# Sharing the last stage's weight loads and result stores between two DMA queues, with whole-row stores for 20 of 36 tiles

## The chip, the cores and the metric
The kernel runs on one core of one Trainium2 chip, in one launch. Its time is that of one execution on the device, in microseconds (us). Times are given as the median of several executions; the profile comes from one execution more, which has a time of its own.

## The reference
Three layers follow one another, all in float32:

```python
# attention with pooled keys and values: q, k, v [8 batches, 8 heads, 576, 64]
k_p = k.reshape(B, H, 72, 8, D).mean(axis=3)
v_p = v.reshape(B, H, 72, 8, D).mean(axis=3)
attn = softmax(q @ k_p^T / sqrt(D));  x = attn @ v_p        # -> x [4608, 512]
# dense layer with a rational activation: w_in [512, 2048], w_out [2048, 512]
h = x @ w_in
P = a[0] + a[1]*h + a[2]*h*h + a[3]*h*h*h
Q = 1 + |b[0]|*|h| + |b[1]|*h*h
x = (P / (Q + 1e-6)) @ w_out                                 # [4608, 512]
# soft mixture of 8 experts with 4 slots each: phi [512, 32], w1 [8, 512, 1024], w2 [8, 1024, 512]
logits = x @ phi
d = softmax(logits, axis=0);  slot_input = d.T @ x           # [8, 4, 512]
slot_out[e] = max(slot_input[e] @ w1[e], 0) @ w2[e]
out = softmax(logits, axis=1) @ slot_out                     # [4608, 512]
```

## The kernel before
The 4608 rows are 36 tiles of 128. A run is four tiles, so there are nine runs, and the dense layer goes through each run in eight pairs of 128-wide blocks of the hidden 2048. For each batch the keys and values are first pooled by matmuls (`pool_k` L471, `pool_v` L477, copies L484) from tiles of `kN` and `kH`, the first of them loaded for batch 0 into slots A and S (L462, L464); for later batches accumulating DMAs on GpSimd's queue pool them in DRAM (`summed`, L429). Scores (L518), the softmax and the second product (L581) follow, then the three-term products of the dense layer (L663 to L665) and the rational function, shared by VectorE, ScalarE and GpSimd (L677 to L701). L737 transposes the results, L754 copies them out of PSUM. Words of w_in and w_out are split into parts by `words` (L597 to L611).

The last stage has two functions. `experts()` (L833) makes the loads of the last stage: 16 of folded w_out blocks (`wod`, 256 KB each, L876), 10 half tiles of the expert weights (256 KB, L860) and 59 whole tiles (512 KB, L891), all on SyncE's queue (`nc.sync`). They need a free slot: the tags q, at, kp, vp, en, x, w, gt, A, S, kv and att name sets of buffers that the body also uses. `tail()` (L893) has the slots of the experts, the transposes of the w_out blocks (L881), the product with them (L959), the first expert layer (L1013), its transposes (L1027) and the second layer (L1045), which is made in two halves of 256 columns, `hf` 0 and 1. For each half the eight groups of matmuls of L1045 are followed by a scaling (`so`, L1089 or L1090), a sum over the groups (`pg`, L1091), a copy (`so4`, L1092), and then the combination: matmuls into `po` (L1106), a copy to an `o` buffer by ScalarE (L1113) or VectorE (L1114) and a store (L1117). A store takes 256 rows by 256 columns, so 256 KB in rows of 1 KB; 36 of them are issued, 18 for each half.

The order of all work is written out. `Plan.op` numbers each group of instructions as the kernel's functions call it (a task). `Plan.run` then emits the tasks one after another as the string `ORDER` (L67 on) names them: "2792,A:0" is task 2792, which takes slot 0 of tag A for its buffer; a letter a, b or c behind the number takes the first, second or third alternative engine of the task. Each engine and each DMA queue works through its own tasks in that order, and a task waits on its engine for all that it depends on, for the reader of the slot's last content too. Task numbers that the steps name: 41 to 44 load the four tiles of batch 0 (41 and 42 of keys, 43 and 44 of values), 45 the half tile; 46 to 48 are `pool_k`, 49 and 50 the copies of L484, 51 to 53 `pool_v`; 119, 126 and 133 load tiles of w_in; 2633 is a group of transposes (L737) of the last run, 2602 and 2632 are copies (L754) that free its bank; 2775 to 2830 are loads of the last stage; 2915 to 2918 are the four groups of the second layer for columns 0 to 255, 2919 to 2922 those for columns 256 to 511.

Of the kernel before, what the change touches and what calls it, by code (L numbers as in the profile page):

```python
# [8 lines left out]
F32 = mybir.dt.float32  # L9
# [3 lines left out]
AF = mybir.ActivationFunctionType  # L13
# [5 lines left out]
B, H, S, D = 8, 8, 576, 64  # L19
SP = 72  # L20
# [13 lines left out]
t_act = lambda n, ps=1, ap=0: (0.172 if ps else 0.205) + 0.085 * ap + 0.000833 * n  # L34
# [18 lines left out]
FILL, FILZ = 30, 0  # L53

# [13 lines left out]
0 1 38 41,A:0 36 2 42,A:2 3 140,kv:1 31 45,S:2 4 32 119,gt:4 5 43,A:1 6 7 8 9 10 11 46,h:0 47 44,A:0 141,gt:3 126,gt:7 55,U:1 142 71,q:1 143 144  # L68
120,t:1 48 145a,w:10 583,kv:1 121 133,kv:0 147,gt:6 584,gt:1 35 122 154,gt:0 51 87,U:2 49 587,gt:5 123 146a 127,gt:4 52 124b,w:9 125a 128a 50 129 53
130 56,h:1,st:1,at:0 54 586,gt:7 131,w:7 72,h:0,st:0,at:1 57 132 134,t:0 59 58 588,wk:0 135a 75 73 37 76 60 136 61 12 13 74 14 15 137 16 77 589 62  # L70
161,kv:0 138a,w:6 155,t:1 103,U:1 585,kv:1 63a 156a 168,gt:4 139 17 148,gt:3 613,q:2 78 18 64,wk:1,att:0 182,gt:2 19 149a 359 20 65a 590 597,q:1 33
79a 66,wk:1 157 591 88,h:0,st:0,at:0 592 150 67 82,wk:0,S:2 89 80,wk:1 83 158 68,r:0,x:1,x:0 81 91 159a,w:2 90 162,gt:0 104,h:1,st:3,at:1 92 69 151 93
160 593,wk:1 107 169,t:0 70 152,w:12 105 170a 108 153 84,r:0 106 163a 94 183,t:1 594 253,gt:3 109 171 95 175,gt:6 85 39 110 231,gt:1 184a 189,kv:1 595
247,gt:7 111a 905,q:0 21 185 596 96,wk:0,att:0 22 86 97 98,wk:1 23 164 99 24 114,wk:0,S:0 172 112,wk:1 115 100,r:0 165 113 186 237,kv:0
598,wk:1,wk:0,st:0,at:0 166b,w:4 101 173,w:13 102 25 176,gt:5 174 599 116,r:0 232,gt:2 601 600 177a 602 26 167 117 27 28 614,wk:0,wk:1,st:1,at:1
248,gt:4 118 233a 178 391,h:1 645,q:2 190,gt:0 179 249a 617 180,w:14 392 234 254,gt:6 181 615 238,t:0 618 393 616 603 250 239a 251 255a 394 240 619
263,gt:7 235 191a 415,h:0 256 395,S:0,A:2,U:0 196,gt:1 629,q:1 241 236 187,w:11 192 416 203,kv:0 396 188 367 620 375 242 417 40 397 398a 360 418 604
400a 399 605 243,wk:1,ks:0 420,A:0 401a 439,h:1 419,S:1,U:1 244a 193 421 245,wk:0 608,wk:1,att:0 422a 440 402 621a 246 403,r:0 441 194b,w:1 609 404
195 197,gt:2 405 29 424a 606,wk:1 442 257 198a 406 425 210,gt:3 607 423 407,r:0 630,wk:0,wk:1,st:1,at:0 444,A:1 408 463,h:0 853,q:1 633 443,S:2,U:2
252 199 409 426 464 446 631 634 445 632 610,wk:1,x:3,x:2 410 635 200 427,r:0 448 624,wk:0,att:0 447 611 217,gt:1 465 625 258 279,kv:1 201,w:0 428 449  # L80
269,gt:0 204,t:0 259,wk:0,ks:0 285,gt:5 636 205a 429 466 264,gt:4 430 265a 202 612 260 431,r:0 261,wk:0 266 30 468,A:3 622,wk:1 361 487,h:1 432 623
267 262 368 467,S:1,U:0 433 646,wk:0,wk:1,st:2,at:1 268 206 211,gt:2 488 470 647 212a 648 450 434 489 649 280,t:1 213 469 490 637 471 451,r:0 281a
626,wk:0 650 472 452 651 511,h:0 207 270,gt:7 473 286,gt:6 453 627 512 454 271a 628 455,r:0 272 638,wk:1,att:0 493,U:1 640,wk:0 362 513 456 641 273
639 34 474 457 642,wk:0 274 224,kv:0 458 208,w:15 275,wk:1,ks:0 214 643 209 475,r:0 644 514 218,gt:3 282 215,w:8 276 369 287a 411,wk:0,gt:0 476
517,U:2 283 413,wk:1,gt:4 216 412 652 414 288 492,A:2 277,wk:1 435,wk:0 311,gt:2 653 477 327,kv:1 225,t:0 284 278a 219 491,S:0 437,wk:1 363 478 436
220 479,r:0 459,wk:0,gt:7 438 221 226a 494a 461,wk:1,gt:1 222,w:3 460 227 496 462 654,wk:0,att:0 495 516,A:0 656,wk:1 228 535,h:1 657 223a 295,kv:0
655 289 515,S:2 658,wk:0 497a 290 229,w:5 301,gt:5 518 873,q:2 291,wk:1,ks:0 480 659 498 481 536 660 296,t:1 482 292 312,gt:6 230 519 293,wk:1 537
499,r:0 294 313a 500 520 483,wk:1 297a 501 302,t:0 485,wk:0 370 502 538 303a 298 484 304 486 299 540,A:3 854,wk:1,wk:0,st:1,at:0 521a 300 539,S:1,U:0
559,h:0 305 503,r:0 542 855 306 328,gt:3 560 504 317,gt:5 541 343,kv:0 857 856 383 561 329a 505 522 858 544 506 307,wk:0,ks:0 859 543 545 523,r:0 562
318,t:1 524 319a 525 677,h:1 308 314 546 320 678 315 564,A:1 321 316 563,S:0,U:1 333,gt:2 330 309,wk:1 323,wk:0,ks:0 322 331 310 566 526 507,wk:1,gt:5  # L90
349,kv:1 324 332 860 527,r:0 509,wk:0,gt:6 344,t:0 528 679 508 529 510 364 565 530 325,wk:0 680 371 326a 547,r:0 567 334,t:1 531,wk:0 568 682,A:2 548
# [1102 lines left out]
```

## Time and profile before

| | us |
|---|---|
| median of 3 runs | 778.95 |
| lowest and highest of them | 777.73 and 782.79 |
| the profiled execution | 774.41 |
| its span, first to last instruction | 772.6 |
| granted TensorE clock over the span | 0.991 |

The profile's first lines give busy time in the span: TensorE 732.3 us (95%), VectorE 657.0 (85%), ScalarE 597.1 (77%), GpSimd 472.2 (61%). PE is TensorE, PEld its weight loads, DVE VectorE, ACT ScalarE, POOL GpSimd; SPq is SyncE's queue. q1 is the DMA queue of SyncE's issues, q0 that of GpSimd's. A row gives, where it is a group of instructions, line, engine, operation, out<-in, shapes and count, then busy time and mean in ns, then the idle time ahead and what ended it. Where times are given, they count from the start of the span.

### The profile page before, as it was taken

Reading aid. Unit: us, or ns where it says so; the run is one execution under the profiler, and the core shown is the slowest. Engines: PE = TensorE matmul, PEld = TensorE weight load, DVE = VectorE, ACT = ScalarE, POOL = GpSimd, SP = SyncE. Lnnn points to the kernel's source line nnn. Section 1 sums busy time; section 2 is a strip of 40 time slices with the busy share of each in tenths; the row PEclk is TensorE's granted clock in tenths of the full one; section 3 lists DMA queues with packets and bytes.
Section 4 is the critical chain, followed back from the end, with each engine's and each line's share of the span. In section 5 each row is a group of like instructions: output and inputs, shape, how many; then the busy total and the mean of one; then the engine's idle time right before and its main releaser. Section 6 shows DMA issues by size and latency. Waiting matters only on the chain.

```text
span 772.6 us, 15833 instructions
## 1 busy us (share of the span) xinstructions
PE 732.3 (95%) x6297; PEld 545.6 (71%) x6297; DVE 657.0 (85%) x985; ACT 597.1 (77%) x998; POOL 472.2 (61%) x288
## 2 busy tenths in 40 slices
PE   8999989999999999999999999999999998899983
PEld 6787757768787876877687677768768766664442
DVE  4999999989999998999999899999999998862132
ACT  3689899968986987898798888878898977772122
POOL 1336756578885998677587868837775877520000
PEclk9999999999999999999999999999999999999997
DMA  9767667465545320101001010001000125999998
GB/s 353 275 216 240 163 194 235 86 108 102 116 65 108 83 54 2 42 1 44 2 8 42 2 63 28 1 16 36 14 2 1 42 97 181 353 334 387 399 354 298
DMA packets 40561, 99.41 MB, mean 129 GB/s; under 512 B 4152, under 2 KB 14392, under 8 KB 40424
## 3 DMA queue, kind: packets, MB, share of 16 engines
q1 hardware_dynamic: 37352, 86.02, 31.1%
q0 software_dynamic: 3136, 12.39, 9.4%
q8 instruction: 49, 0.80, 0.4%
q14 instruction: 24, 0.20, 0.1%
HBM read 84.76 MB, written 27.79 MB: 146 GB/s over the span
## 4 chain that ended last, share of the span: by engine, by line
PE 57%; DVE 19%; ACT 12%; DMA 4%; issue 3%; POOL 3%; SPq 0%; DVEq 0%; ACTq 0%; POOLq 0%
PE h L663 12%; PE h L665 11%; PE h L664 11%; DVE a L685 4%; PE sc L518 4%; PE pt L569 3%; PE av L581 3%; PE bank L711 3%; DVE r L699 2%; DVE a L701 2%; DVE u L697 2%; PE l L1013 2%; ACT r L696 2%; ACT s L677 2%; ACT a L679 2%
## 5 line engine op out<-in xcount | busy, mean ns | idle before, releaser
L663 PE MATMUL h<-xh,wh 128*128 128x512 f32 x576 | 241.7, 420 | 9.5 <-DVE a L685 3.9
L664 PE MATMUL h<-xl,wh 128*128 128x512 f32 x576 | 227.4, 395 | 0.1
L665 PE MATMUL h<-xh,wh 128*128 128x512 f32 x576 | 227.4, 395 | 0.0
L682 POOL TENSOR_TENSOR a<-a,s 128x1024 f32<-128x1024 f32 (+1 forms) x67 | 158.1, 2359 | 84.4 <-ACT s L677 57.6
L690 POOL TENSOR_TENSOR u<-u,s 128x1024 f32<-128x1024 f32 (+1 forms) x71 | 164.8, 2321 | 30.6 <-ACT s L687 25.5
L663 PEld LDWEIGHTS h<-xh,wh 128*128 128x128 f32 x576 | 108.3, 188 | 44.0 <-issue 7.8
L665 PEld LDWEIGHTS h<-xh,wh 128*128 128x128 f32 x576 | 108.3, 188 | 25.8
L664 PEld LDWEIGHTS h<-xl,wh 128*128 128x128 f32 x576 | 108.7, 189 | 19.4 <-DVE xl L586 0.5
L696 ACT ACTIVATE r<-s 128x512 f32<-128x512 f32 x144 | 87.1, 605 | 29.3 <-DVE a L701 28.6
L697 DVE SCALAR_TENSOR_TENSOR u<-u,r 128x512 f32<-128x512 f32 x144 | 96.9, 673 | 15.1 <-ACT r L696 14.2
L699 DVE SCALAR_TENSOR_TENSOR r<-a,cs,r 128x512 f32<-128x512 f32 x144 | 107.4, 746 | 0.0
L685 DVE SCALAR_TENSOR_TENSOR a<-h,cs,a 128x1024 f32<-128x1024 f32 (+1 forms) x75 | 92.7, 1236 | 10.3 <-ACT u L681 6.6
L701 DVE SCALAR_TENSOR_TENSOR a<-u,r 128x512 f32<-128x512 f32 x144 | 98.0, 682 | 3.2
L679 ACT ACTIVATE a<-h,cs 128x1024 f32<-128x1024 f32 (+1 forms) x73 | 85.8, 1176 | 9.7 <-PE h L665 9.5
L693 ACT ACTIVATE s<-u,cc 128x1024 f32<-128x1024 f32 (+1 forms) x75 | 84.1, 1121 | 7.7 <-POOL u L690 7.7
L688 POOL TENSOR_SCALAR s<-u,gb 128x1024 f32<-128x1024 f32 (+1 forms) x57 | 68.5, 1202 | 22.6 <-ACT u L681 12.4
L681 ACT ACTIVATE u<-h 128x1024 f32<-128x1024 f32 (+1 forms) x75 | 74.2, 990 | 8.0 <-PE h L665 3.4
L677 ACT ACTIVATE s<-h 128x1024 f32<-128x1024 f32 (+1 forms) x75 | 74.1, 989 | 5.6 <-PE h L665 5.1
L722 DVE STREAM_TRANSPOSE G<-a 128x1024 f32<-128x1024 f32 x56 | 69.3, 1238 | 0.1
L560 POOL TENSOR_TENSOR at<-at,st 128x576 f32<-128x576 f32 x31 | 36.9, 1192 | 22.5 <-DVE st L552 14.7
L537 ACT ACTIVATE at<-sc,st 128x72 f32<-128x72 f32 x192 | 45.4, 335 | 5.6 <-DVE st L531 5.2
L569 PE MATMUL pt<-ident,at 128*72 128x128 f32 x288 | 41.4, 273 | 3.6 <-DVE xl L586 1.5
(219 smaller groups left out, 1084.1 us busy)
## 6 DMA issues: line engine op xcount, KB each, us to landing
wx<-in_w SPq DMA_DIRECT2D x49, 512.0 KB, 5.9
qt<-in_qT SPq DMA_DIRECT2D x36, 256.0 KB, 2.9
out_dram<-o SPq DMA_DIRECT2D x22, 256.0 KB, 3.2
G<-in_w_in SPq DMA_DIRECT2D x10, 512.0 KB
G<-in_w_out SPq DMA_DIRECT2D x10, 512.0 KB, 5.6
G<-in_w SPq DMA_DIRECT2D x10, 512.0 KB, 8.1
wx<-wod SPq DMA_DIRECT2D x16, 256.0 KB, 4.0
ks<-in_kU POOLq DMA_DIRECT2D x7, 576.0 KB, 5.7
```

What stands on the lines that cost most here:

```text
L663: p_.matmul(o, w[:, 0, k], xh[r].t[:, k], start=(k == 0), stop=False)
L664: p_.matmul(o, w[:, 0, k], xl[r].t[:, k], start=False, stop=False)
L665: p_.matmul(o, w[:, 1, k], xh[r].t[:, k], start=False, stop=(k == 3))
L677: op("ACT", t_act(n), lambda fl=fl: a_.activation(out=fl(S_), in_=fl(h), func=AF.Square), [pt_(h)], [pt_(S_)], c, after=was("sq"), also=[A ...
L679: op("ACT", t_act(n, 1, 2), lambda fl=fl: a_.activation(out=fl(A), in_=fl(h), func=AF.Identity, scale=a3, bias=a2), [pt_(h), abt], [pt_(A) ...
L682: mul = lambda eng, fl=fl: eng.tensor_tensor(out=fl(A), in0=fl(A), in1=fl(S_), op=ALU.mult)
L685: op("DVE", t_dve(n, 1), lambda fl=fl: v_.scalar_tensor_tensor(out=fl(A), in0=fl(h), scalar=a1, in1=fl(A), op0=ALU.mult, op1=ALU.add), [pt ...
L690: mul = lambda eng, fl=fl: eng.tensor_tensor(out=fl(U), in0=fl(U), in1=fl(S_), op=ALU.mult)
L696: op("ACT", t_act(512, 0), lambda f=f, q=q: a_.activation(out=q.t, in_=S_.t[:, f], func=AF.Exp, scale=-1.0), [(S_, f)], [q], c + ky(r, "EX"))
L697: op("DVE", t_dve(512), lambda f=f, q=q: v_.scalar_tensor_tensor(out=U.t[:, f], in0=U.t[:, f], scalar=QC, in1=q.t, op0=ALU.add, op1=ALU.mult),
L699: op("DVE", t_dve(512, 1), lambda f=f, q=q: v_.scalar_tensor_tensor(out=q.t, in0=A.t[:, f], scalar=a0, in1=q.t, op0=ALU.add, op1=ALU.mult) ...
L701: op("DVE", t_dve(512), lambda f=f, q=q: v_.scalar_tensor_tensor(out=A.t[:, f], in0=U.t[:, f], scalar=-2.0, in1=q.t, op0=ALU.add, op1=ALU. ...
```

## The change
The change does four things. `wod` loads (L876), whole-tile loads (L891) and stores (L1117) get GpSimd's queue as an alternative to SyncE's. `FULL = 16`: for the row tiles from 16 on (20 of 36) the copies of both halves go into one `o` buffer [128, 2, 512] and the store is made once, in `hf` 1, as 512 KB in rows of 2 KB; the buffers live from the first half to the second. Their copies are split by 256 columns, so the 30 copies become 42, and the 36 stores become 26 (16 of 256 KB, 10 of 512 KB). L599 gets GpSimd as an alternative. And all of `ORDER` is replaced, by 3039 entries instead of 3037, of which the first difference is the third entry.

In the new order the alternatives are used as follows: 22 of the 59 whole-tile loads on GpSimd's queue and 37 on SyncE's, `wod` loads 0 of 16, L599 0 of 32, half-row stores 10 of 16, whole-row stores 6 of 10. The new numbers of the last tasks differ from the old ones, since there are more copies and fewer stores.

```diff
+FULL = 16
...
-0 1 38 41,A:0 36 2 42,A:2 3 140,kv:1 31 45,S:2 4 32 119,gt:4 5 43,A:1 6 7 8 9 10 11 46,h:0 47 44,A:0 141,gt:3 126,gt:7 55,U:1 142 71,q:1 143 144
...
-2689 2691,r:0 2633,wk:1 2855 2793,S:1 2692 2634 2856 2857 2776,w:5 2858 2693 2795,A:1 2663,wk:1,gt:6 2792,A:3 2690 2782,q:1 2694 2664 2665,wk:0,gt:5
...
+0 1 31 41,A:2 32 37 2 42,A:3 35 3 140,kv:1 45,S:0 4 38 43,A:0 5 36 6 7 8 9 10 11 12 13 46,h:1 141,gt:1 47 44,A:2 142 119,gt:3 126,gt:4 143 55,q:1 144
...
+2685 2633,wk:0 2661 2842 2792,A:0 2843 2687,wk:1 2662 2844 2735 2845 2846 2686 2744 2780a 2688 2847 2848 2776,w:5 2849 2691,r:0 2689 2795,A:1 2850
...
+2902 2906,U:0 2812a,gt:0 2907,wk:1 2815a,A:1 2915,r:0 2909,U:2 2910 2908 2821a,A:0 2894,m:1 2911,wk:1 2913,wk:0 2916 2912,U:2 2914 2917 2822a,gt:2
+2828,att:0 2918 2826a,gt:3 2919,wk:1 2945,t:0 2946,r:0 2825,kv:0 2920 2827,S:1 2947,t:1 2824,gt:5 2830,w:4 2984,wk:0,r:0 2829,A:0 2982,h:0 2986,w:14
...
-        op("ACT", 0.67, lambda: a_.activation(out=t.t, in_=raw.t[:, :, 1].bitcast(F32), func=AF.Abs, scale=2.0**-112), [raw], [t], key)
+        op("ACT", 0.67, lambda: a_.activation(out=t.t, in_=raw.t[:, :, 1].bitcast(F32), func=AF.Abs, scale=2.0**-112), [raw], [t], key,
+           alt=[("POOL", 1.25, lambda: g_.tensor_scalar_mul(t.t, raw.t[:, :, 1].bitcast(F32), 2.0**-112), False)])
...
-                    op("SP", SPI, lambda o=o, f=f: nc.sync.dma_start(out=o(), in_=wod[f].t), [wod[f]], [(b, part)], key, nbytes=128 * 2048)
+                    put = lambda eng, o=o, f=f: eng.dma_start(out=o(), in_=wod[f].t)
+                    op("SP", SPI, lambda put=put: put(nc.sync), [wod[f]], [(b, part)], key, nbytes=128 * 2048, alt=[("POOL", 1.0, lambda put=put: put(nc.gpsimd), False)])
...
-                op("SP", SPI, lambda o=o, src=src: nc.sync.dma_start(out=o(), in_=src), [], [(b, part)], key, nbytes=128 * 4096)
+                put = lambda eng, o=o, src=src: eng.dma_start(out=o(), in_=src)
+                op("SP", SPI, lambda put=put: put(nc.sync), [], [(b, part)], key, nbytes=128 * 4096, alt=[("POOL", 1.0, lambda put=put: put(nc.gpsimd), False)])
...
+        whole = {}
...
-                    o = buf(["w", "gt"], [128, 2, n, 256], "o", np_=2)
+                    full = g >= FULL
+                    if full and hf == 0:
+                        whole[g, jj] = buf(["w", "gt"], [128, 2, 512], "o", np_=4) if n == 1 else [buf(["w", "gt"], [128, 2, 512], "o", np_=4) for _ in range(2)]
+                    o = whole[g, jj] if full else buf(["w", "gt"], [128, 2, n, 256], "o", np_=2)
...
+                        if full:
+                            for m in range(n):
+                                oo = lambda i=i, m=m, os=os, po=po, cols=cols: os[m].t[:, :, cols] if len(po) == 1 else os[m].t[:, i, cols]
...
+                                op("ACT", t_act(w // n), lambda oo=oo, pm_=pm_: a_.activation(out=oo(), in_=pm_(), func=AF.Copy), [po[i]], [prt], kk,
+                                   alt=[("DVE", t_dve(w // n), lambda oo=oo, pm_=pm_: v_.tensor_copy(oo(), pm_()), False)])
+                            continue
...
+                        if full:
+                            if hf == 1:
+                                put = lambda eng, o=os[m], r0=r0: eng.dma_start(out=out[r0 : r0 + 256, :].rearrange("(j p) d -> p j d", p=128), in_=o.t)
+                                op("SP", SPI, lambda put=put: put(nc.sync), [os[m]], [], kk, nbytes=128 * 4096, alt=[("POOL", 1.0, lambda put=put: put(nc.gpsimd), False)])
+                            continue
+                        put = lambda eng, o=o, m=m, r0=r0, cols=cols: eng.dma_start(out=out[r0 : r0 + 256, cols].rearrange("(j p) d -> p j d", p=128), in_=o.t[:, :, m])
+                        op("SP", SPI, lambda put=put: put(nc.sync), [o], [], kk, nbytes=128 * 2048, alt=[("POOL", 1.0, lambda put=put: put(nc.gpsimd), False)])
```

## Rows read from the trace of the kernel before

**Rows 1.** The page's 40 equal slices: DMA busy tenths, and GB/s.

```profile
DMA  9767667465545320101001010001000125999998
GB/s 353 275 216 240 163 194 235 86 108 102 116 65 108 83 54 2 42 1 44 2 8 42 2 63 28 1 16 36 14 2 1 42 97 181 353 334 387 399 354 298
```

**Rows 2.** Busy time by stretches; PE, PEld, DVE, ACT, POOL, clock, DMA share, GB/s.

```profile
28.00:140.00 112.00, 105.94 (x798) 80.00 (x796) 107.69 (x169) 102.25 (x165) 61.77 (x43) 1.00 0.68 208
140.00:580.00 440.00, 433.25 (x3800) 332.77 (x3800) 411.95 (x606) 374.09 (x639) 334.01 (x188) 1.00 0.20 44
660.00:680.00 20.00, 16.99 (x140) 13.40 (x139) 16.37 (x26) 15.85 (x29) 12.03 (x10) 1.00 0.86 315
678.00:678.60 0.60, 0.60 (x19) 0.41 (x17) 0.46 (x1) 0.60 (x2) 0.41 (x1) 1.00 0.00 0
680.00:700.00 20.00, 19.27 (x186) 13.82 (x188) 13.32 (x30) 12.29 (x29) 1.43 (x3) 1.00 1.00 383
700.00:740.00 40.00, 36.48 (x377) 16.99 (x369) 6.35 (x13) 8.27 (x17) 0.00 (x0) 1.00 1.02 391
766.00:772.60 6.60, 0.00 (x0) 0.00 (x0) 0.00 (x0) 0.00 (x0) 0.00 (x0) 0.50 0.69 231
```

**Rows 3.** The chain that ended last, from 740 us: start, us, what.

```profile
735.99 8.60 DMA wx<-in_w
744.64 3.64 PE lo L1045 x58
...
749.34 1.86 PE lo L1045 x32
```

**Rows 4.** Timeline of SyncE's queue: start, us, line, operation, count.

```profile
671.87 1.28 SPq L891 DMA_DIRECT2D wx<-in_w  x3
...
678.13 0.80 SPq L891 DMA_DIRECT2D wx<-in_w  x2
```

**Rows 5.** The chain that ended last, from 0 to 60 us.

```profile
10.16 2.81 PE pk L477 x4
13.06 0.41 ACT kp L484
13.51 2.43 PE pk L477 x4
...
17.50 1.19 PE sc L518 x8
...
32.32 1.73 PE pv L477 x4
```

**Rows 6.** Timeline of ScalarE, TensorE and GpSimd near 680 us.

```profile
678.73 0.59 ACT L754 ACTIVATE G<-gp 128x512 f32<-128x512 f32 x1
...
681.74 0.66 PE L737 MATMUL gp<-ident,a 128*128 128x128 f32 x4 [0.37 <-ACT G L754]
...
678.91 1.27 POOL L690 TENSOR_TENSOR u<-u,s 128x512 f32<-128x512 f32 x1 [0.51 <-ACT s L687]
```

**Rows 7.** Timeline of GpSimd: the issue of one DMA.

```profile
143.83 1.06 POOL L429 DMA_DIRECT2D vs<-in_vS  x1
```

**Rows 8.** DMA queue by window 724:737, 764:770, 151.2:152.4: packets, MB, share.

```profile
q1 hardware_dynamic: 1444, 5.26, 101.6%
...
q1 hardware_dynamic: 2133, 2.05, 102.6%
...
q1 hardware_dynamic: 129, 0.23, 51.4%
```

**Rows 9.** VectorE's timeline at 754 us, and copies of 735:773 by line and shape.

```profile
754.24 1.29 DVE L1114 COPY o<-po 128x512 f32<-128x512 f32 x2 [0.55 <-PE po L1106]
...
L1114 DVE COPY o<-po 128x1024 f32<-128x1024 f32 x2 | 2.5, 1225 | 1.7 <-DMA wx<-in_w 1.7
L1114 DVE COPY o<-po 128x256 f32<-128x256 f32 x2 | 0.8, 416 | 0.0
L1113 ACT ACTIVATE o<-po 128x256 f32<-128x256 f32 x2 | 0.8, 380 | 1.1 <-PE po L1106 1.1
```

**Rows 10.** Page, DMA queues over the span: packets, MB, share of 16 engines.

```profile
q1 hardware_dynamic: 37352, 86.02, 31.1%
q0 software_dynamic: 3136, 12.39, 9.4%
```

More of the change, by code (lines that the diff above doesn't have):

```diff
@@ L72 @@
[L72 to L79, printed above, removed]
@@ new lines @@
+71,U:0 587,gt:2 145a,w:10 583,kv:1 133,kv:0 48 584,gt:5 146 51 120,gt:0 121 122 14 127,t:0 52 123 49 50 128 147,gt:3 124b,w:6 129 53 125a
+56,h:0,st:0,at:1 54 130 154,gt:0 87,U:1 72,h:1,st:1,at:0 131a,w:13 57 58 588,wk:1 59 134,gt:6 132 75 73 135a 76 74 60 589 77 161,kv:1 136 61 137 62
+138a,w:8 585,kv:0 103,q:1 155,gt:7 168,gt:4 63a 15 148,t:1 182,gt:1 139 16 78 17 149a 18 156 64,wk:0,S:1 79a 590 65a 19 591 20 150 66,wk:0 592 157
+88,h:1,st:2,at:1 67 158 82,wk:0,S:0 91 80,wk:1 159a,w:15 586,gt:0 83 89 68,r:0,x:2,x:3 359 92 169,t:0 39 90 81 160 151 104,h:0,st:3,at:0 93 69
@@ new lines @@
+593,wk:0 597,q:1 162,gt:5 231,gt:7 105 152,w:7 70 163a 107 153 84,r:0 106 170a 108 94 109 594 33 85 110 95 183,t:1 86 595 184a 175,gt:0 164 237,kv:0
+21 613,q:0 111a 596 96,wk:1,att:0 22 97 185 98,wk:0 23 171 99 114,wk:1,S:1 115 112,wk:0 172 100,r:0 113 165 247,gt:4 186 189,kv:1
+598,wk:0,wk:1,st:2,at:0 101 166b,w:9 253,gt:1 176,gt:3 167 102 24 173,w:12 25 601 116,r:0 232,gt:2 599 602 174 177a 600 26 117 27
+614,wk:1,wk:0,st:1,at:1 248,gt:5 118 233a 28 178 391,h:1 249a 179 238,t:0 234 190,gt:6 392 615 180,w:1 617 254,gt:0 616 181 393 618 239a 250 191a
@@ new lines @@
+218,gt:4 369 411,wk:0,gt:1 476 225,t:0 283 276 517,U:0 216 413,wk:1,gt:6 652 295,kv:0 412 311,gt:5 288 414 284 653 492,A:0 477 277,wk:1 435,wk:0 278a
+219 491,S:1 437,wk:1 363 478 436 220 479,r:0 459,wk:0,gt:3 438 221 226a 494a 222,w:4 461,wk:1,gt:2 460 495 496 654,wk:0,att:0 462 516,A:2 227 656,wk:1
+535,h:1 228 655 289 327,kv:1 657 497a 229,w:5 658,wk:0 515,S:2 223a 291,wk:1,ks:0 498 480 518 301,gt:4 290 481 536 659 375 312,gt:7 482 292 660
+296,t:1 293,wk:1 537 230 499,r:0 519 294 297a 483,wk:0 500 370 302,t:0 317,gt:0 313a 501 485,wk:1 520 303a 538 502 484 298 486 304 540,A:3
@@ new lines @@
+670 715,r:0 747,S:0,A:3,U:0 716 671 717 748 672 718 374 732 697 673 750 719 674 733,r:0 749 675 765,h:1 734 676 766 752 735 698,gt:0
+874,wk:1,wk:0,st:1,at:0 753 736 767 877 875 664 876 768 377 878 751 879 890,wk:0,wk:1,st:3,at:1 771,U:1 872 880 787,h:0 769,S:2,A:0 891 881 893
+737,r:0 892 788 894 770 738 720,gt:1 895 882,wk:1,att:0 772 884,wk:0 883 789 739 885 754 740 906,wk:1,wk:0,st:2,at:0 896 755,r:0 790 1149,q:2 774a 897
+909 1133 910 1115,q:0 907 1130,ks:0 886,wk:0 773 775 792,A:2 741 908 791,S:1,U:2 756 898,wk:1,att:0 911 757 809,h:1 794 899 758 887 912 900,wk:1 810
@@ new lines @@
+1126a 962 1124 824 946 786,gt:4 825,r:0 1127,wk:0,x:1,x:0 945 826 963 1128 827 842 380 1129 964 828 948 947 843,r:0 1150,wk:0,wk:1,st:2,at:1
+965,S:0,A:0,U:0 949 844 983,h:1 966 1140 1151 984 845 1152 1141 1153 846 985 1154 808,gt:5 968 847,r:0 986 967 848 849 950 1144,wk:0,att:0 807 850 970
+1145 969 829 987,S:2,A:2,U:1 971 851 852,gt:7 951,r:0 1142,wk:0 921 1005,h:0 924a,L:0 1143a 988 952 1146,wk:0 922,m:0 972 953 990 954 1006 830,gt:6
+955,r:0 1147 1007 381 956 923 1148 989 387 991 927,wk:1 928,wk:0 1008 930 992 929,en:0 957 958 931,h:1,wk:1,wk:0 1010,kv:0 993 1155 932 973,r:0
@@ new lines @@
+1528 1475 1451 1493,r:0 1442 1452 2925 1510 1454 1543,h:1 1453 1527 1494 1681,wk:1,wk:0,st:3,at:0 2926 1530 1544 1904,q:1 1495 1664 1935 1682 1531
+1545 1684 1683 1496 1529 1511,r:0 1546 1685 1512 1675,wk:1,att:0 1686 1549,U:1 1673,wk:0 1565,h:0 1513 1676 1687 1532 1674a 1566 1514 1547,S:2,A:1
+1498,gt:1 1677,wk:1 1515,r:0 1548 1516 1567 2927 1937 1678 1550 348 1517 1476,gt:0 1568 1518 1497 1679 1552 1533,r:0 1519 1551 1571,U:2
+1890,wk:1,wk:0,st:2,at:1 1553 1570,A:3 1534 1587,h:1 1535 1569,S:1 1893 1536 1588 1894 1572 1891 1520,gt:2 1537,r:0 1589 1892 1538 1554 1574 1539
@@ new lines @@
+1690,wk:0,att:0 1688,wk:1 1691 1540 1590 1689 1575 1573 1555,r:0 1692,wk:1 1592,A:0 1556 1542,gt:3 1609,h:0 1591,S:0,U:0 1895 1936a 1594 1610 1693
+2192,ks:0 1593 1557 1919,q:2 1694 1611 1558 1896 1595 1559,r:0 1612 1596a 1560 1576 1905,wk:1,wk:0,st:0,at:0 1561 1597 1562 1713,h:1 1614,A:2
+1564,gt:4 1577,r:0 1714 1613,S:2,U:1 1578 1908 1615 1616 1906 1715 1579 1909 1580 1541 1598 1563 1617 1618 1581,r:0 1897,wk:0,att:0 1716 1898 1582
+1619 1907 1583 1899,wk:0 1584 1735,h:0 1900 1910 1599,r:0 1718,kv:0 1901,wk:1,x:2,x:3 1600 1911 1601 1717,S:1,U:2 1736 1602 1902 1720 1586,gt:5
@@ L203 @@
+2990,h:1 3010a 3031a 3009a 2991a,gt:6 3012a 3020,h:0 3011 2994,r:0,wk:0 3022,w:13 3021,gt:4 2996a,w:4 2974,h:0 2995a 3032,h:1 2997 3035,r:0,wk:1 3033a
+2998 3037 2975a 2976a 3023a 3036a 3024 3003,wk:0,r:0 3002 3034a 3004,w:2 3005a 3038a 3006 2993 3007a 2992a
 """
```

233 lines of the change are left out of this document (105 added, 128 removed).

## The prediction

> **What bounds the kernel now.** I read the page's 40 slices first, for the one engine that is not busy throughout: the DMA engines work hard in the first third, are nearly idle through the middle, and run at nine tenths or more over the last eight slices, some 150 us [rows 1]. Then busy time by stage: up to 680 us TensorE leaves 6.06 us of 112 and 6.75 us of 440 free, so the body is bound by compute, with the DMA engines at a fifth. From 680 us on it turns over: DMA share 1.00 and more, 383 and 391 GB/s, while the other engines run out of work [rows 2]. The chain that ended last says the same: it waits 8.60 us for a weight tile that lands at 744.6, does the last matmuls of the second expert layer, and everything behind is copies and stores [rows 3]. In SyncE's queue I then look for the place where the loads stop being issued: three 512 KB loads go out by 671.87 + 1.28 = 673.15, the next two at 678.13 [rows 4]. At 678.0 to 678.6 nothing was moved at all, 0 GB/s [rows 2]. So three things set the time: the compute up to 680, the moment at which the bulk of the weights can start, and the bytes from there to the last store.
>
> **Head.** The new order issues the load of the first value tile of batch 0 (task 43) fifth and no longer sixth, and moves the first 512 KB tile of w_in (119) behind it. TensorE began on that tile at 10.16 us, and the three groups of `pool_v` then set the chain to the scores at 17.50 [rows 5]. 512 KB fewer in front at the 353 GB/s of the first slice [rows 1] are 524,288 B / 353 GB/s = 1.49 us: −1.5. At best the first two groups also shrink to the 1.73 us that four such matmuls take at 32.32: 2.81 + 2.43 − 2 × 1.73 = 1.8 more, −3.3, rounded to −3.5. At worst the gain is eaten because the ACT copies of L484 now stand behind one group more, two of 0.41 us [rows 5]: +0.8, rounded to +1. I take −1.5, since what follows is chained to the scores.
>
> **Body, 28 to 660 us.** The whole order of 3037 entries is replaced, yet the same instructions stay on nearly the same engines: the new POOL alternative of L599 is used 0 times in 32, L688 goes from 57 to 60 on POOL, L601 from 3 to 5 on DVE, and so on by twos and threes. TensorE's idle time is all there is to win here, 6.06 + 6.75 us [rows 2], and a fresh order can lose as much as it wins. I take 0, with half of the first figure, ±3, as bounds.
>
> **Where the loads start again.** Before, the loads issued up to 673.15 came to 13.0 MiB; the queue went on at 678.13 [rows 4]; that sum is counted along the order. In the new order SyncE issues 12.75 MiB up to a like point and then stands at task 2792, whose slot A:0 is freed by task 2633, a group of transposes (L737) that ended at 681.74 + 0.66 = 682.4 before [rows 6]. There it had waited for an L754 copy; its bank in the new order is free after the L754 copy that ended at 678.73 + 0.59 = 679.3, so it can end near 680. What SyncE carries behind 2792 waits with it. GpSimd's queue doesn't help earlier: its first load of this part (2780) stands behind its last compute, which ended at 678.91 + 1.27 = 680.2 [rows 6]. So the restart is some 680 against 678.13, and the bytes left are 23.25 MiB against 23.0 (0.26 MB at 375 GB/s = 0.7 us). Were the engines dry in between, this costs 1.9 + 0.7 = 2.6; loads still in flight cover a part, as they did before until shortly ahead of 678.0. I take +2.0; below, 0, if the loads issued later than I think cover it; above, +5.0, with A:0 as late as before (4.3 + 0.7).
>
> **The bulk of the weights.** Before, 23.0 MiB = 24.1 MB landed between 679 and 744.6, 368 GB/s over all, in stretches of 383 and 391 [rows 2]; 375 between them is my rate for both kernels, 65 us. Twenty-two of the 59 loads of 512 KB move to GpSimd's queue. Its compute is over by then, so nothing waits there but stores. The issue itself costs 1.06 us on GpSimd [rows 7] against about 0.4 on SyncE (0.80 for two, [rows 4]); 22 × 1.06 = 23 us lies inside 65 and beside SyncE's. Stores of the first half of the columns, seven of eight, also go through GpSimd, and the last loads (2822, 2826) stand behind matmuls in the same queue: +0.5, between 0 and three issues of 1.06 us, +3. Before, one queue already filled the engines (101.6% share at its best, 406 GB/s over 13 us, [rows 8]), so a second queue adds no bandwidth that the rows show.
> The Trainium skill ("DMA: Bandwidth & Descriptors" in its section "Issuing engines are not separate DMA queues") says that transfers issued by several engines run on the same 16 DMA engines, and that issuing from several saves only sequencer time. That speaks against any gain from the sharing; by that rule the sharing is worth 0 here, against the −4.9 us of the first rival below, and the trace's full share with one queue agrees.
>
> **After the last weight.** Before, from the last landing (744.64) to the end of the span (772.6) it was 28.0 us; the first copy for the second half of the columns ran from 754.24 on DVE, its store could go out at 755.0 [rows 9]. Stores of the first half covered the gap. Now only 16 of 36 tiles store half rows in the first half (8 × 256 KB = 2.1 MB); the other 20 keep both halves in ten buffers and go out once as ten stores of 512 KB. Behind the last landing I count: last group of the second layer, 32 matmuls, 1.86 us; 751.2 to 755.0 for the scaling, the group sum and the first combination, 3.8 [rows 3, 9]; about 0.9 from issue to bytes (after the issue of 678.13 nothing had moved by 678.6 [rows 2, 4], so over 0.5); together 6.6, in which 2.1 MB of first-half stores take 2.1 / 342 GB/s = 6.1 [rows 8] and just fit. Then 8 × 256 KB at 342 = 6.1 and 5.24 MB in 2 KB rows. Their price: at 342 GB/s as 1 KB rows 15.3 us, at 406 as the 4 KB weight rows [rows 8] 12.9; I take 376 between, 13.9. Then 2.1 us from the last bytes to the end, as before: the share of 0.69 of the last 6.60 us [rows 2] is 4.5 us of transfers, to 770.5. 6.6 + 6.1 + 13.9 + 2.1 = 28.7 against 28.0: +0.7. The whole rows save about 1.4 us of transfer, and moving 2.6 MB of stores from the covered gap behind it takes more than that back. Twelve more copies (416 and 380 ns for 256 columns, 1225 ns for 1024 at once, [rows 9]) amount to a few us on two engines and lie beside 20 us of stores. Should they come first, each costs 0.4 us.
>
> **Sum.** −1.5 + 0 + 2.0 + 0.5 + 0.7 = +1.7. The profiled execution took 774.41 (span 772.6 and 1.8 around it), which makes 776.1; the median of the three runs lies 4.5 above the profiled one, and I give the time beside that: 778.95 + 1.7 = 780.6.
>
> **The rivals.**
> Two queues move more than one. For: in two windows one queue made 383 and 406 GB/s [rows 2, 8], so the mean is not the ceiling. Against: the share is at 1.00 in both. 24.4 MB at 406 instead of 375 take 60.1 instead of 65.0 us, −4.9: 775.7. With no lag at the restart either it would be 773.7.
> The other side, slower: GpSimd's queue moves a byte slower than SyncE's. The only rows for it are the accumulating loads of the pooling, 12.39 MB for 9.4% of 772.6 us = 72.6 us of all engines, 171 GB/s [rows 10] (q1: 86.02 MB for 31.1%, 358 GB/s). 17.3 MB move over (22 loads, 16 stores). At 171 they take 101.2 us instead of 46.1 at 375: +55, 836 us. They add to what lies in DRAM, which plain loads don't, and that speaks against taking the figure over; half way, 273 GB/s, is +17, 798 us. It decides from about 331 GB/s down (+6.1, over 1%).
> A:0 comes as late as in the trace of before, 682.4: +3.0 on the forecast, 783.6.
> The new order of the body wins or loses the half of TensorE's idle time, 6 us: 774.6 or 786.6.
> The change doesn't do what it says: 2 KB rows cost per byte what 1 KB rows cost, the 1.4 us go: 782.0. The one stretch with such rows, 0.23 MB at a share of 51.4%, is too short to exclude it [rows 8].
>
> **How the numbers follow.** Forecast 0.46; two queues faster 0.16; GpSimd's queue slower 0.12; late slot 0.10; body 0.10 (either side half); dear 2 KB rows 0.06. One per cent is 7.8 us, about what a measurement of this kernel can tell from no change. Under 771.2 come 0.05 of the forecast (head and start at their good ends), 0.07 of the two queues and 0.05 of the body: 0.17. Over 786.7 come 0.09 of the slow queue, 0.03 of the body, 0.04 of late slot and forecast: 0.16. The rest, 0.67, is within 1%. The range: the terms' good ends (−3.5, −3, 0) with part of the faster queues reach to 769; their bad ends (+1, +3, +5, +3, not all at once) to 789. Outside lie the slow queue below some 320 GB/s and a combination of all good ends, about 0.2.
>
> **What would show it.** TensorE's scores first at about 16 and no longer 17.50. SyncE's queue with a pause from 672 to between 679.5 and 682, and a DMA share of 660 to 680 of some 0.73 instead of 0.86. q0 (GpSimd's) at 29.7 MB and its share: near 17.3 MB / 375 added, 46 us or 6%, on the 9.4%; clearly more would be the slow queue. Last weight at 746 to 747; first whole-row store some 10 us after it; span about 774.3. The forecast is wrong if the DMA rate from 680 on leaves 360 to 390 GB/s, if PE idle from 28 to 660 changes by over 3 us, or if the tail behind the last weight is not 27 to 31 us.

## The result and the profile after

| | before | changed |
|---|---|---|
| median of 5 runs, us | 778.95 (777.0 to 782.79) | 782.74 (779.24 to 783.91) |
| ratio to the kernel before, 95% interval | | 1.0053 (1.003 to 1.0076) |
| measured again later, 6 runs of the changed kernel | 777.98 | 784.15; 1.0073 (1.0051 to 1.0094) |
| profiled execution; span, us | 774.41; 772.6 | 782.74; 780.8 |
| granted TensorE clock | 0.991 | 0.976 |

The changed kernel is slower by 0.5 to 0.7%, some 4 to 6 us, which is within 1%. One execution in all the experiments, of the old head with the changed rest, took 1437.62 us and is left out of its ratio. The two profiled executions stand 8.2 us apart, more than the medians: the one of before lies 4.5 us under its median. So the split by stages below is of 8.2 us, and how much of each part is the kernel and how much the luck of one execution is what the experiments are to tell.

Page of the changed kernel, 40 slices and the DMA queues, against [rows 1, 10]:

```profile
DMA  8657587564536230101011010000200024989989
GB/s 321 237 199 238 128 240 246 122 112 87 114 67 125 55 82 2 28 1 36 23 43 41 2 49 1 1 29 15 71 2 14 15 83 135 376 325 399 403 301 326
...
q1 hardware_dynamic: 27112, 68.71, 25.3%
q0 software_dynamic: 7968, 29.69, 15.3%
```

The first slices move less than before (321 and 237 GB/s, before 353 and 275), and the last slice but one has a dip to 301 where [rows 1] has 354. q0 carries 17.3 MB more, as counted, and its share of the engines' time grows from 72.6 us (9.4% of 772.6) to 119.5 (15.3% of 780.8): 46.9 us, 369 GB/s, near the 375 that I took for SyncE's queue. So the rival with the slow queue is out at once.

Busy time by stretches of the changed kernel (columns as in [rows 2]):

```profile
28.00:140.00 112.00, 106.30 (x777) 80.96 (x778) 103.55 (x167) 96.64 (x157) 59.98 (x43) 0.96 0.70 216
140.00:580.00 440.00, 433.77 (x3755) 334.35 (x3762) 412.51 (x606) 374.22 (x641) 336.11 (x191) 1.00 0.22 47
...
684.00:688.00 4.00, 4.00 (x38) 4.00 (x38) 3.56 (x6) 3.94 (x8) 3.10 (x3) 1.00 0.28 77
...
700.00:740.00 40.00, 39.26 (x416) 19.43 (x418) 8.92 (x24) 10.28 (x22) 9.62 (x19) 1.00 1.02 402
...
752.00:756.00 4.00, 3.48 (x40) 1.96 (x32) 1.39 (x3) 2.00 (x6) 2.05 (x3) 1.00 0.56 196
756.00:760.00 4.00, 3.58 (x34) 2.68 (x34) 2.95 (x7) 1.70 (x5) 1.52 (x3) 1.00 0.72 255
```

TensorE is as busy in the body as before (433.77 of 440 against 433.25), but its clock from 28 to 140 is 0.96 instead of 1.00. The gap in the loads near 678 is now near 686 (share 0.28). And from 752 to 760, where the stores should run, the engines lie idle for 0.44 × 4 + 0.28 × 4 = 2.9 us; before, the shares there were 0.96 and 1.03:

```profile
752.00:756.00 4.00, 3.09 (x36) 2.12 (x36) 2.05 (x4) 2.43 (x4) 0.00 (x0) 1.00 0.96 319
756.00:760.00 4.00, 3.10 (x41) 2.26 (x36) 1.38 (x2) 3.40 (x6) 0.00 (x0) 1.00 1.03 343
```

The chain that ended last, first in the head (against [rows 5]), then at the end (against [rows 3]):

```profile
1.36 5.29 PE bank L390 x26
6.65 5.96 PE pk L472 x40
12.62 3.61 PE pk L478 x4
...
16.45 1.73 PE pk L478 x4
...
20.21 1.19 PE sc L519 x8
...
735.26 7.04 DMA G<-in_w
...
742.35 1.91 PE lo L1049 x26
744.26 4.25 PE po L1114 x46
748.51 1.86 PE lo L1049 x32
750.38 1.06 PE po L1114 x8
751.44 1.86 PE lo L1049 x32
```

The scores begin at 20.21 instead of 17.50: the load that was moved forward is no longer waited for, but `pool_v` begins 2.5 us later and its first group takes 3.61 us. Ahead of it the chain is TensorE's own work alone: 26 filler matmuls (L390; 22 before) and then `pool_k` (L472). The second expert layer ends at 753.30, only 2.1 us later than before, and from there to the end it is 27.5 us against 21.4.

SyncE's queue in the changed kernel, one issue of GpSimd, and SyncE's waits from 670 to 690 (waited for: us in total, times, longest):

```profile
678.57 7.81 SPq L894 DMA_DIRECT2D wx<-in_w  x3
...
686.05 0.33 SPq L894 DMA_DIRECT2D wx<-in_w  x1
686.42 0.91 SPq L878 DMA_DIRECT2D wx<-wod  x2
...
757.64 0.39 SPq L1136 DMA_DIRECT2D out_dram<-G  x1
...
727.42 0.53 POOL L894 DMA_DIRECT2D wx<-in_w  x1 [2.45 <-DMA wx<-in_w]
...
SPq L894 <- PE gp L739: 3.4, 1, 3.4
```

Here is the stop that was expected: SyncE waits 3.4 us for transposes (L739, which is L737 of before) and goes on at 686.05, with the third of the three loads that the first line merges. The first store of the second half, a whole-row one, goes out only at 757.64.

From the same traces, by stage (us; "product" is the dense layer's first matmul line; "last weight" is the end of the last 4 KB packet of a weight, read from the packet records):

| | before | changed | difference |
|---|---|---|---|
| end of the first product | 46.5 | 53.3 | +6.8 |
| first to last product | 625.1 | 624.8 | −0.3 |
| last product to restart of the loads | 6.5 | 8.0 | +1.5 |
| restart to last weight | 66.1 | 63.7 | −2.4 |
| last weight to the end of the span | 28.4 | 31.0 | +2.6 |

The five differences make the 8.2 us.

### The profile page after: what moved, and what is told of

Read it like the earlier page. It is cut to its first block, busy times and chain, and to the rows that moved or that the text cites. A ratio compares the mean times of both kernels' runs of the same rounds, so it can differ in the third digit from the quotient of the medians.

```text
span 780.8 us, 15860 instructions
## 1 busy us (share of the span) xinstructions
PE 742.7 (95%) x6297; PEld 555.7 (71%) x6297; DVE 654.8 (84%) x990; ACT 592.0 (76%) x998; POOL 500.1 (64%) x333
## 3 DMA queue, kind: packets, MB, share of 16 engines
q0 software_dynamic: 7968, 29.69, 15.3%
## 4 chain that ended last, share of the span: by engine, by line
PE 59%; DVE 14%; ACT 10%; POOL 7%; DMA 5%; issue 4%; SPq 0%; POOLq 0%; DVEq 0%; ACTq 0%
PE h L665 12%; PE h L667 11%; PE h L666 11%; PE sc L519 3%; PE pt L570 3%; DVE a L687 3%; PE av L582 3%; PE bank L713 2%; POOL u L692 2%; POOL a L684 2%; PE po L1114 2%; ACT a L681 2%; PE pss L811 2%; DVE r L701 2%; DMA wod<-wo 2%
## 5 line engine op out<-in xcount | busy, mean ns | idle before, releaser
L684 POOL TENSOR_TENSOR a<-a,s 128x1024 f32<-128x1024 f32 (+1 forms) x66 | 155.4, 2355 | 92.6 <-ACT s L679 65.7
L698 ACT ACTIVATE r<-s 128x512 f32<-128x512 f32 x144 | 87.2, 606 | 28.4 <-DVE a L703 27.3
L690 POOL TENSOR_SCALAR s<-u,gb 128x1024 f32<-128x1024 f32 (+1 forms) x60 | 71.7, 1194 | 26.4 <-ACT u L683 16.9
```

The source lines that it names most:

```text
L684: mul = lambda eng, fl=fl: eng.tensor_tensor(out=fl(A), in0=fl(A), in1=fl(S_), op=ALU.mult)
L698: op("ACT", t_act(512, 0), lambda f=f, q=q: a_.activation(out=q.t, in_=S_.t[:, f], func=AF.Exp, scale=-1.0), [(S_, f)], [q], c + ky(r, "EX"))
```

## The experiments

Ratios are to the kernel before, measured beside each experiment on the same chip; its medians there were 777.0 to 778.0. "The first dense products" at 51.7, 52 and 58.2 us in the expectations is the end of the eighth one; below I give the start of the first.

**The head taken over, both ways.** All tasks up to the first dense product in the order of the other kernel, the rest unchanged (free slots were taken where the named one was still in use):

```diff
-0 1 31 41,A:2 32 37 2 42,A:3 35 3 140,kv:1 45,S:0 4 38 43,A:0 5 36 6 7 8 9 10 11 12 13 46,h:1 141,gt:1 47 44,A:2 ...
+0 1 38 41,A:0 36 2 42,A:2 3 140,kv:1 31 45,S:2 4 32 119,gt:4 5 43,A:1 6 7 8 9 10 11 46,h:0 47 44,A:0 141,gt:3 ...
```

> The changed kernel, but everything up to the first product of the dense layer in the order of the kernel before. Theory 1 (the head: TensorE's clock was granted at half in two stretches before 37 us and the first dense products came 6.4 us late): they come at 52 us again, and the time falls from 782.7 by 4 to 6 us, to 777 to 779, no slower than before. Theory 2 (the two profiles differ by luck in the head, and the cost is the tail, where the DMA engines are dry between 752 and 760): it stays at 782 to 783, ratio 1.004 to 1.006.

Measured: 781.92 us, 1.0061 (1.0038 to 1.0085). Not faster than the changed kernel.

> The kernel before, but everything up to the first product of the dense layer in the order of the changed kernel. Theory 1 (the head costs the time): 783 to 785, ratio 1.005 to 1.008, with the clock at half in parts of 5 to 40 us. Theory 2 (the tail costs it): 779, ratio 0.998 to 1.002.

Measured: 779.05 us, 1.0022 (1.0004 to 1.004). So the new head costs 1.7 us (0.3 to 3.1) in the old rest, and taking it out of the changed kernel gave back nothing that could be measured (the intervals are wide enough to hide 2 us). Theory 1 is wrong as the main cause, and the profile shows why one pair of executions misled: with the old head the first product began at 45.97, 47.91, 47.91, 49.77, 50.02 and 50.68 us in six profiles, so the profile of before is the earliest of them. With the new head it began at 52.66 to 54.02 in six. The later start is real, 4.8 us in the mean; in this kernel 2.1 us of it are made up before the last product (623.0 us from first to last instead of 625.1).

The clock has a large part in the start. The stretch from 28 to 36 us in three kernels, one after the other: the kernel before; the old rest with the new head; the changed kernel with all on one queue (told of below):

```profile
28.00:36.00 8.00, 8.00 (x66) 5.47 (x64) 7.60 (x16) 7.42 (x15) 3.17 (x3) 1.00 0.65 240
```

```profile
28.00:36.00 8.00, 6.54 (x28) 5.95 (x29) 5.73 (x9) 1.45 (x4) 2.67 (x3) 0.50 0.73 260
```

```profile
28.00:36.00 8.00, 7.50 (x33) 6.74 (x34) 5.43 (x11) 1.40 (x3) 1.88 (x2) 0.50 0.85 319
```

With the new head the clock is at half, 1.2 GHz, over this whole stretch in six of six profiles, and TensorE, though busy for 6.5 to 7.5 of the 8 us, gets through 28 to 33 matmuls instead of 66. With the old head it was full in four of six and 0.79 in the other two. Ahead of this fall TensorE had run two groups of 16-column matmuls (`pool_k`) one behind the other; in the old order ten matmuls of 128 columns that serve only as filler (L389) stand between them.

Within one head, too, the start follows TensorE's pace. In every profile the first filler matmuls come 0.21 us apart, and later ones 0.11. The record of the clock has its first entry where the full pace begins (a stretch ahead of it is printed as 1.00): with the old head at 4.3, 5.4, 5.2, 6.3, 6.7 and 17.7 us, for the six starts in the order above. In the last of these `pool_k` ran at half pace throughout; its 32 matmuls in the kernel before and in that profile:

```profile
5.29 3.64 PE L471 MATMUL pk<-wide,kvn 128*128 128x16 f32 x32
```

```profile
6.22 6.85 PE L472 MATMUL pk<-wide,kvn 128*128 128x16 f32 x32
```

Where the full pace began at nearly the same time, at 6.7 us with the old head and 6.6 with the new, the first product began at 50.02 and 53.36. So the new head is later by more than this luck, some 3 us.

**The fillers alone, both ways.** Five filler tasks put between the two groups in the changed kernel, and moved from there in the kernel before:

```diff
-... 10 11 12 13 46,h:1 ... 588,wk:1 59 ...
+... 10 11 46,h:1 ... 588,wk:1 12 13 14 15 16 59 ...
```

> The changed kernel; only five filler tasks (10 matmuls of 128 columns) stand where the kernel before has them, between the two groups of 16-column matmuls near 24 us, and no longer ahead of them and behind. In three of three profiles with the new head the clock fell a second time at 26 to 28 us, in three of three with the old head it did not. Theory (the fall comes from the missing fillers and is what the new head costs): no second fall, the first dense products 1.5 to 3 us earlier than the 58.2 us of the changed kernel, and 780 to 781 instead of 782.7. Rival (the order of the loads in the head costs it): the fall goes, the time stays within 0.5 us of the changed kernel's.

Measured: 780.97 us, 1.005 (1.0028 to 1.0071).

> The mirror of it: the kernel before, with the five filler tasks moved from between the two groups of 16-column matmuls to behind the second. Theory: the clock falls at 26 to 28 us and the time goes up by 1 to 3 us, ratio 1.001 to 1.004. Rival: no fall or no cost, ratio 0.999 to 1.001.

Measured: 777.85 us, 1.0008 (0.9993 to 1.0023).

The same stretch of the first and of the second:

```profile
28.00:36.00 8.00, 7.35 (x53) 6.38 (x54) 6.78 (x14) 2.88 (x6) 1.89 (x2) 0.79 0.84 302
```

```profile
28.00:36.00 8.00, 7.98 (x59) 7.23 (x60) 6.59 (x12) 3.79 (x8) 1.91 (x2) 0.79 0.91 345
```

The fall did not go, it became shorter, and the first product began at 50.8 us; the mirror fell too, as two of the six profiles of the old head did. The time did not move beyond its interval either way: 780.97 is what the theory named, but beside its own kernel before it is 1.005, against 1.0053 and 1.0073 of the changed kernel. The place of the fillers has a part in how long the fall lasts; that it is what costs time is not shown.

**Two queues without the rest, and the rest on one queue.** In the first, 22 of the last 38 whole-tile loads of the old order go out on GpSimd's queue; in the second, the letter a is struck from all loads and stores of the changed order:

```diff
-2777,A:2 2700,m:2 2698a 2778 2701,L:0 ...
+2777,A:2 2700,m:2 2698a 2778a 2701,L:0 ...
```

> The kernel before with its order and its half-row stores; only 22 of the last 38 loads of 512 KB go out on GpSimd's queue. If the 16 DMA engines are the limit and SyncE's queue fills them alone: 779, ratio 0.998 to 1.002, the last weight within 1 us of 744.6 and 390 GB/s from 700 to 740. Rival (two queues fill them better, as the 402 GB/s of the changed kernel's profile in 700 to 740 may say): last weight 2 to 4 us earlier, ratio 0.995 to 0.997. Rival (GpSimd's queue is the slower one): last weight later by over 2 us.

Measured: 781.6 us, 1.007 (1.0046 to 1.0094).

> The changed kernel with its order, but all loads and stores of the last stage on SyncE's queue, in the same places of the order. If the sharing is worth nothing: 782 to 783.5, ratio to the kernel before 1.004 to 1.007. If two queues move more, or free SyncE from waiting at a late slot: slower than the changed kernel by 2 to 4 us, 785 to 787.

Measured: 782.39 us, 1.0079 (1.0051 to 1.0107).

700 to 740 us with two queues in the old order and, below it, the end of its loads; then its waits on SyncE's queue; then the changed order on one queue:

```profile
700.00:740.00 40.00, 34.22 (x344) 14.48 (x346) 5.85 (x13) 5.64 (x13) 7.41 (x14) 0.99 0.98 376
...
740.00:744.00 4.00, 2.92 (x20) 1.29 (x16) 0.42 (x1) 0.47 (x1) 0.53 (x1) 0.69 0.59 186
...
SPq L894 <- PE lo L1049: 14.4, 1, 14.4
```

```profile
700.00:740.00 40.00, 38.71 (x404) 19.22 (x406) 9.17 (x25) 10.22 (x23) 1.19 (x2) 1.00 1.03 404
```

Two queues move no more than one: 402 GB/s in the changed kernel, 404 in the same order on one queue. In the old order they move less, 376 against 391 [rows 2]. Not because a byte costs more there: each queue waits for its own next free slot, SyncE's once for 14.4 us (its longest wait for a slot in this stretch before was 5.8), and from 740 to 744 the engines are idle for 0.41 × 4 = 1.6 us. The second layer then ends 10 us behind the last weight (756.5 against 746.5) instead of 7.0, and from the last weight to the end it takes 31.9 us. So the order of slots decides whether a split queue hurts: it cost 0.7% in an order that was laid out for one queue, and in the new order, laid out for two, one queue is not measurably different.
The Trainium skill ("DMA: Bandwidth & Descriptors", "Issuing engines are not separate DMA queues") says that transfers run on the same 16 DMA engines whichever engine issues them; 402 and 404 GB/s agree. It says that only the sequencer's time to issue is saved; here that was worth nothing measurable, 1.0079 on one queue against 1.0053 and 1.0073 on two.

**Whole rows.** "Cover" means the stores of the first half that keep the DMA engines busy while the second half is still being computed. First two splices that tell little. One had the kernel before up to the tail and the changed order from there, on one queue; the other the changed kernel up to the tail and the old order of the tail, with half rows on both queues.

> The kernel before up to the tail, with whole-row stores for 20 tiles and the changed kernel's order of the tail, all on SyncE's queue. Theory (the stores of the first half run out as cover): a stretch of 2 to 3 us with idle DMA engines between the last weight and the first store of the second half, and from the last weight to the end 29 to 31 us instead of 28.4; ratio 1.000 to 1.003. Rival (2 KB rows are worth more than the lost cover): ratio 0.997 to 0.999.

Measured: 788.55 us, 1.0131 (1.0112 to 1.0151).

> The changed kernel up to the tail, with all 36 stores in half rows, ordered as in the kernel before, and 22 of them on GpSimd's queue. Theory (the whole rows cost the cover): no idle stretch of the DMA engines behind the last weight, last weight to end 28 to 29 us instead of 31.0, and 780 to 781. Rival (the second queue costs it, not the rows): last weight to end stays at 30 to 31, 782 to 784.

Measured: 790.45 us, 1.0174 (1.0148 to 1.0199).

Both tell of the splice and not of the rows: in the first a group of the second half of the layer stood ahead of the first half's combination, so that TensorE waited 4.77 us for a weight and no store went out until 753.29 (748 to 752: 0 GB/s); in the second TensorE waited 5.11 us for a copy. Nothing follows from them but that the order around the stores costs more than the form of the stores.

The same question put better: every copy and store in its own place of the old order, on one queue, with `FULL` alone changed (and the stores of the first half left out for whole tiles):

```diff
+FULL = 16
...
-                    o = buf(["w", "gt"], [128, 2, n, 256], "o", np_=2)
+                    o = whole[g, jj] if full else buf(["w", "gt"], [128, 2, n, 256], "o", np_=2)
```

> The kernel before in its own order and on one queue, with whole-row stores for 20 tiles: each copy and store stands where that of the kernel before stood, and the 10 stores of the first half fall away. Theory (lost cover): from the last weight to the end 29.5 to 31.5 us instead of 28.4, idle DMA engines before the first store of the second half, ratio 1.001 to 1.004. Rival (2 KB rows are worth it): 27 to 28 us, ratio 0.998 to 0.999.

Measured: 782.29 us, 1.0055 (1.0036 to 1.0075). From the last weight to the end 34.0 us.

> The same with whole rows for 12 tiles. Theory: enough cover is left, the 2 KB rows save 0.5 to 1 us, ratio 0.999 to 1.000. Rival (any store taken out of the first half costs its bytes behind the last weight): ratio 1.001 to 1.002.

Measured: 780.53 us, 1.0021 (1.0002 to 1.0041). From the last weight to the end 31.3 us.

The tail with 20 whole tiles, then with 12:

```profile
748.00:752.00 4.00, 4.00 (x59) 2.26 (x53) 1.16 (x3) 0.66 (x2) 0.00 (x0) 1.00 0.32 109
752.00:756.00 4.00, 3.09 (x36) 1.96 (x34) 2.18 (x5) 2.17 (x5) 0.00 (x0) 1.00 0.00 0
...
764.00:772.00 8.00, 0.00 (x0) 0.00 (x0) 0.00 (x0) 0.00 (x0) 0.00 (x0) 0.50 1.03 369
```

```profile
748.00:752.00 4.00, 4.00 (x62) 2.34 (x64) 1.81 (x3) 0.00 (x0) 0.00 (x0) 1.00 0.69 235
...
756.00:760.00 4.00, 3.09 (x40) 2.13 (x38) 2.43 (x5) 2.52 (x5) 0.00 (x0) 1.00 0.26 93
```

This is the cover, alone. With 20 whole tiles the engines have nothing to do for (0.68 + 1.00) × 4 = 6.7 us between the last weight and the first store of the second half, with 12 for (0.31 + 0.74) × 4 = 4.2 us. The whole rows themselves are cheaper: by the packet records one of 2 KB takes 89 ns and two of 1 KB 97, so 342 GB/s of the half rows [rows 8] become some 373 (the 369 of the row above mixes 2.2 MB in 2 KB rows with 0.8 in 1 KB rows). That doesn't make up for the idle time. With 20 whole tiles the tail is 5.6 us longer than before, and the way from the last product to the last weight 1.3 us shorter (71.3 against 72.6), since fewer stores go out ahead of it; the 4.3 us left agree with the 0.55%. The tail of the first came out longer than its theory said (29.5 to 31.5 us); for 12 tiles the rival's ratio fits, and not the gain of the theory.

**The changed kernel with more cover.** `FULL = 24` in the changed kernel, four more stores in the first half; beside it the changed kernel itself.

> The changed kernel once more, beside the next three on the same chip. The ratio to the kernel before was 1.0053 (1.003 to 1.0076); 1.003 to 1.008 is expected. Head: the first dense product between 53 and 55 us as in the three profiles with the new head. From the last weight to the end 30.5 to 31.5 us, with 2.5 to 3.5 us of idle DMA engines in it.

Measured: 784.15 us, 1.0073 (1.0051 to 1.0094); first product at 53.36, 30.7 us from the last weight to the end.

> The changed kernel with whole-row stores for 12 tiles instead of 20: four more stores of 256 KB (1.05 MB) go out in the first half of the columns. Theory (the 2 to 3 us come from the lost cover): the idle of 2.9 us between 752 and 760 goes to under 1 us, from the last weight to the end 29 us, and 1.5 to 2 us less than the changed kernel on the same chip. Rival (the time in the tail is the copies of 256 columns or GpSimd's issues): the same time as the changed kernel within 0.5 us.

Measured: 785.12 us, 1.0093 (1.007 to 1.0117). The tail:

```profile
752.00:756.00 4.00, 4.00 (x60) 2.61 (x54) 0.69 (x1) 2.09 (x4) 1.96 (x3) 1.00 0.91 329
756.00:760.00 4.00, 2.69 (x28) 1.54 (x25) 1.71 (x4) 1.56 (x4) 1.77 (x4) 1.00 0.85 288
768.00:772.00 4.00, 2.75 (x18) 1.85 (x16) 1.38 (x4) 0.38 (x1) 0.00 (x0) 0.50 0.80 272
772.00:776.00 4.00, 2.07 (x6) 1.17 (x6) 1.54 (x3) 0.60 (x1) 2.14 (x3) 0.50 0.64 228
```

The first gap shrank as expected, from 2.9 to 1.0 us, but a new one opened behind it, (0.20 + 0.36) × 4 = 2.2 us from 768 to 776, and 31.5 us from the last weight to the end are no gain. The 1.5 to 2 us that were expected did not come. TensorE runs at half clock there and does 6 matmuls in 4 us, but so it does in the changed kernel from 768 to 772, whose DMA engines are full (1.03). That the stores wait for the chain of combination and copy, which the new order hands out late, is argued and not shown. None of the twelve kernels beats the kernel before.

## Why the prediction was right, and where its steps were not

The time, 780.6 for a measured 782.74, within 1%, came out nearly right: +1.7 was forecast, +3.8 measured. That is not because each step held. In the pair of profiles the head came out 8.3 us worse than forecast (+6.8 for −1.5), the way from the last product to the last weight 3.4 better (−0.9 for 2.0 + 0.5) and the tail 1.9 worse (+2.6 for +0.7); errors of opposite sign made the sum look better than its terms.

**Head, −1.5: wrong in sign.** The step said that TensorE waits for the tile which is now loaded earlier. It does not wait for it any more, but `pool_v` starts later all the same, because the chain there is TensorE's own work, much of it at half pace. The bounds of −3.5 to +1 left out that a re-ordered head changes what TensorE runs ahead of a fall of the clock, though [rows 5] showed groups of 2.81 and 2.43 us next to one of 1.73. Measured: the first product 4.8 us later in the mean of six profiles each (some 3 at like pace), and in time +1.7 us (0.3 to 3.1) in the old rest, nothing measurable in the new.

**Body, 0: right.** First to last product 624.8 us against 625.1, and 624.6 to 626.0 in the others with either rest but the one told of above (623.0).

**Restart of the loads, +2.0: right, and for its reason.** Last product to restart 8.0 us against 6.5, with SyncE's wait on the transposes as the row that ends it. The rival with slot A:0 as late as in the trace of before (+5.0 for this term) did not happen.

**The bulk, 375 GB/s for both, and +0.5 for stores in front: too dear.** Restart to last weight took 2.4 us less than before, the weights alone at 24.4 MB / 63.7 us = 383 GB/s. Not because of the queue (404 on one queue). The term for stores in front came out the other way: by the packet records 0.83 MB of stores went out ahead of the last weight before, and 0.23 MB in the changed kernel, and 0.6 MB less at 378 GB/s are 1.6 us. With these stores counted the rate was 378 GB/s before and 386 in the changed kernel; what makes the rest of the difference is open. From last product to last weight, the lag included, it was 72.6 us before, 71.7 and 72.5 in two profiles of the changed kernel, and, without the two splices, 71.7 to 73.4 over six profiles of the changed rest against 71.3 to 72.6 over five of the old rest on one queue. So most of the lag is made up before the last weight.

**Tail, +0.7: the mechanism right, the size off.** The working held that 2.1 MB of first-half stores "just fit" into a gap of 6.6 us behind the last weight, 5.7 of it until the first store of the second half is issued. That store went out 7.9 us behind the last weight (757.64 − 749.78), the engines ran dry for 2.9 us, and the term measured +2.6 and, in the second profile, +2.3. The term that was too small is the last group of 32 matmuls, taken as 1.86 us behind the last weight: the layer ended 3.5 us behind it (753.30 − 749.78). It did not wait for that weight at all. In the chain TensorE runs from 742.35 on without a pause, with 46 and 8 matmuls of the first half's combination (L1114) ahead of the last groups. The steps from there to the store took 4.3 us instead of 3.8. The rest of the working held: from the issue of that store to the end it was 23.2 us, and 0.9 + 6.1 + 13.9 + 2.1 = 23.0 were forecast; 2 KB rows came to 373 GB/s where I took 376. On one queue the same order had a tail of 29.0 us, but its last weight came 73.0 us after the last product, so the two sums, 102.1 and 102.7, differ little.

**The rivals.** Two queues faster: out (402 and 404 GB/s). GpSimd's queue slower: out, 369 GB/s over all that was moved to it, 0.53 to 0.75 us for an issue instead of the 1.06 that I charged; that its use can still cost 0.7% through the order of slots was in none of the rivals. 2 KB rows no cheaper: out. The body: out.

**By parts.** In the old kernel the new head costs 0.2%, two queues 0.7% and 20 whole-row tiles 0.55%; all of it together with the new order costs 0.5 to 0.7%. If the parts simply added up, about 0.8% would be taken back by the order, which was laid out for these queues and buffers; that they add up was not shown, and what in the order does so was not tried piece by piece. The lost cover is shown as a cost in the old order; in the changed kernel more cover brought nothing, so that it is what the changed kernel loses is not shown.

## What to carry to other kernels

A store that is taken out of a stretch in which it was covered and put into one in which it is the bound must be priced at its whole transfer plus the idle time that it leaves behind, and the cheaper row is set against that. Splitting loads between two queues brings nothing once one queue keeps the DMA engines at a share of 1.00, and can cost when the order in which slots come free was laid out for one. Before a few us are read off one pair of profiles, look at the same stage in several executions: here the first product moved by 4.7 us under one and the same order of the head.

## What the runs showed of the hardware that was not expected

GpSimd's queue carried plain loads at the rate of SyncE's, though the only rows of before for that queue stood at 171 GB/s. The two queues of the changed kernel from 700 to 740 us:

```profile
q0 software_dynamic: 2508, 9.16, 57.5%
q1 hardware_dynamic: 2023, 6.84, 44.3%
```

Over their shares of 40 us these are 398 and 386 GB/s. The start of the kernel is not repeatable to a few us: with the same order of the head, TensorE ran at half pace in the first 20 us for stretches of different length, and the first product began anywhere from 45.97 to 50.68 us.
